# New engine orders for an attention and token-mixing kernel, its split last tile moved to the end of TensorE's list, and the tile's second half run as whole matmuls

## The chip, the cores and the metric

The kernel runs on one core of a Trainium2 chip. The metric is the device time of one execution in microseconds (us), measured over runs of the same program; it is compared between the kernel before and the kernel after. A difference of about half a per cent is the least that such a comparison can tell from none.

The engines have their own instruction lists and meet through semaphores: TensorE (PE, with its weight loads as PEld), VectorE (DVE), ScalarE (ACT), GpSimd (POOL) and SyncE (SP), which here only issues transfers.

## The reference

Two branches of one block read the same input x of 2048 tokens by 448 features and are mixed by a gate per token.

```python
def _A_ref(x, wq, wk, wv, wo, beta):          # 16 heads of 28, four segments of 512 tokens
    ...
    phi = lambda t: jnp.where(t > 0, t + 1.0, jnp.exp(t))
    ...
    for s in range(N):
        logits = jnp.einsum('bhqd,bhkd->bhqk', qs, ks) * scale + mask
        a_dot = jnp.einsum('bhqk,bhkd->bhqd', _softmax(logits, axis=-1), vs)
        ...
        a_mem = num / den                     # phi(q) @ M and phi(q) @ z, from the segments before
        o = g * a_mem + (1.0 - g) * a_dot
        M = M + jnp.einsum('bhld,bhle->bhde', pk, vs)
        ...
    return o @ wo

def _B_ref(x, w1, b1, w2, b2):                # an MLP over the tokens
    h = _layernorm(x, axis=-1)
    u = _gelu(jnp.einsum('bsd,sf->bdf', h, w1) + b1)
    return (jnp.einsum('bdf,fs->bds', u, w2) + b2).transpose(0, 2, 1)

g = _sigmoid((x * gate_w).sum(-1, keepdims=True))
return g * _A_ref(x, ...) + (1 - g) * _B_ref(x, ...)
```

## The kernel before

The program is a list of some 1,360 named steps. Each step knows its engine, what it reads and writes, and which PSUM bank it takes. `ORDER` is a table, written out by hand into the kernel, that says for every engine in which order its steps stand; `plan` reads it, and `finalize` turns dependencies into semaphore waits. Nothing is reordered at run time: each engine runs its list, and stops at a step whose inputs aren't there. In the table `u0-3*4` stands for the four steps u0-3 to u0-6, `@5` gives the PSUM bank that a step takes, and `#1` marks the second step of a name.

The names of the steps that matter here:

- `pr`, `lo`: projections to keys (k), queries (q) and values (t), on PE. `lo` are two matmuls of 64 rows side by side that begin two tiles at once; `pr` are the whole matmuls that end each of them. `prx`/`cpk1_3`/`cpq1_3` belong to the fourth group of heads, whose rows are gathered later.
- `cpk`, `cpq`, `cpv`: the copies of those results out of PSUM, on ACT or DVE (L703, L719, L765, L789 and others). `gt` is the gate's tanh. Some steps may stand on either engine; the table decides.
- `ek`, `mk`, `phk` and `eq`, `mq`, `phq`: the feature map phi of keys and queries (exponential on ACT, L748 and L772; then DVE).
- `sc0_0` to `sc7_4`: 40 scores steps (L942). Each fills the same four PSUM banks 0 to 3 with matmuls of 28 rows. `exp` (ACT, L951) reads the four banks in one instruction, and `mask` (POOL, L954) zeroes the triangle.
- `pv0` to `pv15`: probabilities times values (L972), in quarter matmuls; then on DVE `ta` (transpose out of PSUM, L986), `rec`, `oa`, `om`, `o` (L1000 on POOL, L1002 on DVE) and `ot` (L1007).
- `mem1` to `mem3` (L1018): phi(q) times the memory, into banks 0 to 3 too, taken out by `tm` on DVE (L1026) before the next scores. `mst` builds the memory.
- `u0` to `u13`: the first MLP product, 16 steps each; `gsq`, `gvh`, `garg`, `gth`, `gelu` work out the gelu.
- `y0` to `y15`: the second MLP product, 14 steps each, one tile of 128 tokens. `y15` is computed in two parts: columns 0 to 319 (`y15-0` to `y15-13`) and 320 to 447 (`y15-0#1` to `y15-13#1`). `wo` is the attention's output product and `ag` the copy that gates it. `fin` (DVE, L1096) adds both branches, and `out` stores them.
- `ldw1`, `ldw2`: loads of the MLP's weights into three slots on SP, each in four parts; `gk`, `gq`: the gathers of the fourth group's heads through a scratch buffer in DRAM; `gk3_h0` and `gk3_h1` bring back the keys of the last segment, which `sc7_2` is the first to read.

A step with mode "x" is either one matmul of 128 columns of weights (whole) or four of 32 columns (quarters, L264). `plan` makes all steps quarters that stand, without a step of narrower rows between, in one run with a `pv` or an `mst`.

Of the kernel before, what the change touches and what calls it, by code (L numbers as in the profile page):

```python
# [21 lines left out]
NFT = 14  # L22
# [266 lines left out]
btr@7 lok0_0 lok0_2 prk0_0 prx0_3 prk0_2 prk0_1 loq1_0@45 lok1_2@67 prk1_2 prq1_0 prq1_1 prx1_3 loq0_2 loq0_0  # L289
loq1_2@45 prq1_2h prq1_2 prq0_2 prq0_2h prq0_1 lot4@45 lot6@67 prq0_0 prt7 prt6 prt5 sc0_0 lok1_0@76 prk1_1 prk1_0  # L290
prt4 sc0_1 lok2_0@57 prk2_1 prk2_0 lok2_2@46 prx2_3 prk2_2 sc0_2 u0-0@5 u1-0@7*2 u2-0@4*2 u1-2*2 u0-1*5 u1-4*3 sc0_3
u0-6*4 u3-0@6*2 u1-7*2 u2-2*2 u0-10 u1-9*2 sc0_4 u2-4*3 u3-2 u0-11*5 u2-7*2 sc1_0 u1-11*5 u4-0@5 u2-9*2 u3-3*3
u4-1*3 u2-11*2 u3-6*2 pv0@7 sc1_1 u2-13*3 u3-8*6 u4-4*2 u3-14 u4-6 u3-15 u4-7*2 u6-0@7 u4-9*2 u5-0@4 u4-11 sc1_2
u4-12 u5-1*2 u4-13*3 u5-3 u6-1 u5-4*2 u6-2 u5-6 pv1@6 sc1_3 u5-7*4 u6-3*9 sc1_4 u5-11 u6-12*4 u7-0@5*3 u5-12*4
u7-3*2 u8-0@6 u7-5*2 sc2_0 u7-7*7 mst0@4 u8-1*3 sc2_1 u8-4*2 pv2@4 u7-14*2 u9-0@7*7 u8-6*2 sc2_2 loq2_0@45 prq2_1
prq2_0 u8-8*3 mem1 loq2_2@54 u8-11*3 prq2_2 u8-14*2 u9-7 prq2_2h u11-0@5*2 u9-8 u11-2*3 sc2_3 u9-9*4 pv3@4 u11-5*2
u10-0@6*2 u9-13*3 sc2_4 u11-7*3 u10-2 u12-0@4*3 u10-3 pv4@7 u12-3 u11-10*3 sc3_0 u11-13*3 u10-4*2 u13-0@7 u10-6*5
u12-4 sc3_1 u10-11*2 u13-1*2 u12-5 u10-13*3 pv5@5 u12-6 u13-3*2 u12-7*4 sc3_2 lot8@56 u13-5*2 u12-11*2 prt8 prt9
u12-13*2 sc3_3 u13-7*3 u12-15 u13-10 wo0#1@6 u13-11*4 mst1@5 u13-15 sc3_4 lok3_0@64 prk3_0 prk3_1 pv6@5 sc4_0
lot10@76 prt10 prt11 pv7@4 wo1@5 sc4_1 lok3_2@67 prk3_2 loq3_0@45 prq3_0 prx3_3 sc4_2 prq3_1 wo3@4 wo2@6 mem2  # L300
y0-0@5*4 y1-0@6*3 y0-4*4 y1-3*2 y0-8 sc4_3 loq3_2@47 y1-5*6 prq3_2 y1-11*2 sc4_4 y0-9 y1-13 y0-10*4 pv8@4 prq3_2h
sc5_0 y3-0@6*7 y2-0@7*3 y3-7 sc5_1 y2-3 wo5@5 y3-8*6 y2-4 sc5_2 y5-0@4*2 y2-5 pv9@5 wo4@6 y2-6 sc5_3 y5-2 y2-7 wo6@5
y2-8 wo7@6 sc5_4 y5-3*2 y2-9*3 y5-5*3 pv10@5 sc6_0 y5-8*3 y6-0@5 y2-12*2 y5-11*2 pv11@6 sc6_1 y5-13 y6-1*7 mst2@4
sc6_2 lot12@67 y4-0@4*2 prt13 y4-2 prt12 mem3 y6-8 y4-3 y6-9 y4-4*3 lot14@67 prt15 prt14 sc6_3 y4-7*5 y6-10*4
y4-12*2 sc6_4 wo8@6 y7-0@5*3 wo9@7 sc7_0 pv12@4 y7-3*4 wo11@6 sc7_1 y7-7*3 y9-0@4 pv13@7 y7-10*4 sc7_2 y8-0@7*4 y9-1
y8-4*4 y9-2*2 sc7_3 wo10@6 y8-8 pv14@5 y8-9*3 sc7_4 y10-0@5 y9-4 y11-0@6*2 y9-5*2 y10-1 y9-7 y8-12*2 y9-8 y11-2*5
y9-9*3 pv15@7 y10-2*3 y11-7*3 y10-5*2 y9-12*2 y11-10*2 y10-7*7 y11-12*2 wo15@7 y15-0@5*5 y15-0#1@6 y15-5*2 y15-1#1
# [36 lines left out]
mask4_2_2#1 mask4_4_1 mask4_4_3 mask4_3_0 mask5_1_1 mask5_0_0 mask5_1_3 mask5_2_2 mask5_2_2#1 o9 mask5_3_0 mask5_4_1
mask5_4_3 o10 mask6_0_0 o11 mask6_1_1 mask6_3_0 mask6_2_2 mask6_1_3 mask6_2_2#1 mask6_4_1 mask6_4_3 o12 mask7_0_0
mask7_1_1 mask7_1_3 mask7_2_2 mask7_2_2#1 o13 mask7_3_0 mask7_4_1 mask7_4_3""",
    "SP": """
dtx0_0 dtx0_1 ldwk0@0 ldwk1 ldwq0@1 ldwqb dtx1_0 dtx1_1 ldx0 ldx4 ldx8 ldbeta ldw1_0_0 dtx2_0 ldx12 dtx2_1 ldw1_0_1
ldw1_1_0 ldw1_0_2 tk0_0 gq0_1 ldw1_2_1 ldw1_1_2 gq0_0 gq0_3 gk0_2 gq0_2 ldw1_2_0 gk0_1 ldw1_1_1 gk0_0 gk0_3 ldw1_0_3
gq0_h1 ldw1_1_3 gq0_h2 gq0_h0 tk0_2 ldw1_3_1 gk0_h1 ldw1_2_2 gk0_h0 ldw1_3_0 ldw1_3_2 tk0_1 ldw1_2_3 gk2_0 tk1_0  # L350
ldw1_3_3 ldwo0 ldwo3 ldw1_4_2 ldw1_4_1 tk0_3 ldw1_4_0 ldwo0b ldwo1 ldw1_5_2 ldw1_5_0 ldwo1b gk2_1 ldw1_5_1 tk1_1
ldw1_5_3 ldw1_4_3 tk1_2 dtx3_0 gk2_2 ldw1_6_0 tk1_3 ldwo2 gq2_0 ldw1_6_1 ldw1_6_2 gq2_1 ldw1_6_3 ldwo2b gq2_3 gq2_2
gk2_3 gq2_h0 gq2_h1 gk2_h1 gq2_h2 ldw2_2_0 ldw2_0_1 dtx3_1 ldw2_2_2 tk2_1 ldw2_0_2 ldw2_1_0 tk2_0 gk2_h0 ldw2_1_1
ldw2_0_3 ldw2_1_2 ldw2_2_3 ldw2_0_0 ldw2_2_1 ldw2_1_3 gq3_3 gk3_3 out1 gq3_0 gq3_2 gk3_0 gq3_1 gk3_1 ldw2_3_0 tk2_3
gk3_2 out0 gq3_h1 gq3_h2 gk3_h0 ldw2_3_1 ldw2_3_3 gk3_h1 tk2_2 gq3_h0 out2 ldw2_3_2 ldw2_4_2 ldw2_5_0 ldw2_4_3
ldw2_4_0 ldw2_4_1 out4 out5 ldw2_6_0 ldw2_5_1 out3 out7 out6 ldw2_7_0 ldw2_5_2 ldw2_7_1 ldw2_5_3 ldw2_6_3 out8
ldw2_7_2 ldw2_7_3 ldw2_6_1 out10 out11 ldw2_6_2 out15 out9 out15#1 out14 out12 out13""",
}


def build_kernel(nc, X, WQ, WK, WV, WO, BETA, W1, B1, W2, B2, GW, OUT):
# [5 lines left out]
    out2 = OUT.rearrange("b s d -> (b s) d")  # L367
# [46 lines left out]
    uT = sb([128, NFT, D])  # L414
# [811 lines left out]
```

## Time and profile before

| | |
|---|---|
| median of 3 runs | 173.53 us (173.21 to 173.86) |
| the profiled execution | 173.38 us, of which 171.7 us are the profile's span |
| PE busy | 165.6 us, 96% of the span |
| DVE busy | 140.2 us, 82% |
| ACT busy | 132.5 us, 77% |
| POOL busy | 60.6 us, 35% |
| DMA | 25.17 MB moved, 147 GB/s on the mean |

The page divides the span into 40 slices, gives the chain of work that ended last, and groups of instructions by line. Its timeline gives for each group of neighbours the start, the duration and, in brackets, how long the engine sat idle before and what ended that. A matmul's shown duration reaches to its modelled end, so neighbouring matmuls overlap in the rows; from start to start shows the pace.

### The profile page before, as it was taken

How to read it: one execution, taken by the hardware profiler on the slowest of the kernel's cores; microseconds unless marked ns; L12 is line 12 of the kernel's file. 1: busy time of each engine (PE TensorE's matmuls, PEld its weight loads, DVE VectorE, ACT ScalarE, POOL GpSimd, SP SyncE). 2: the span in 40 equal slices, each digit the busy share in tenths (PEclk: the TensorE clock that was granted, in tenths of full speed). 3: DMA queues.
4: the chain of work that ended last, by engine and by line, in shares of the span. 5: the costliest groups of instructions: out<-in, count | busy, mean ns of one | idle time of the engine just before them, and what ended most of it. 6: DMA issues, size and time to landing. Idle time of an engine off the chain costs nothing.

```text
span 171.7 us, 5711 instructions
## 1 busy us (share of the span) xinstructions
PE 165.6 (96%) x2415; PEld 79.7 (46%) x2419; DVE 140.2 (82%) x322; ACT 132.5 (77%) x165; POOL 60.6 (35%) x94
## 2 busy tenths in 40 slices
PE   8799999999999999999999999999999999999992
PEld 2235333445444544544454335444544444566650
DVE  3088999979989899999999999987987777986103
ACT  0269999999999999999999998999895898501110
POOL 5000226441340009524255271467343848400000
PEclk9999999999999999999999999999999999999999
DMA  6999995779895695610539900173346150574212
GB/s 145 260 263 288 240 207 156 211 199 223 201 209 157 162 169 132 201 32 15 144 103 203 289 4 0 39 109 115 96 126 197 49 174 28 168 227 122 85 38 80
DMA packets 52632, 25.17 MB, mean 147 GB/s; under 512 B 17134, under 2 KB 52366, under 8 KB 52606
## 3 DMA queue, kind: packets, MB, share of 16 engines
q1 hardware_dynamic: 51814, 24.22, 57.7%
q10 hardware_dynamic: 792, 0.58, 1.7%
q8 instruction: 19, 0.31, 0.9%
q14 instruction: 7, 0.06, 0.1%
HBM read 18.76 MB, written 2.36 MB: 123 GB/s over the span
## 4 chain that ended last, share of the span: by engine, by line
PE 85%; DVE 5%; SPq 5%; DMA 3%; issue 1%
PE t L264 71%; PE t L942 7%; PE t L972 5%; SPq L516 4%; DMA t<-in_A_x_dram 3%; DVE t L885 2%; DVE t L1026 1%; PE t L825 1%; SPq L506 1%; PE t L1018 1%; DVE t L719 1%; DVE t L1096 0%; DVE t L752 0%; SPq L510 0%; DVE t L763 0%
## 5 line engine op out<-in xcount | busy, mean ns | idle before, releaser
L264 PE MATMUL t<-t 128*32 128x448 bf16 (+8 forms) x1650 | 141.7, 347 | 2.1 <-DMA t<-in_A_wv_dram 0.8
L264 PEld LDWEIGHTS t<-t 128*32 128x32 bf16 (+2 forms) x1654 | 64.8, 97 | 64.7 <-issue 14.1
L951 ACT ACTIVATE t<-t 128x2048 bf16<-128x2048 f32 x40 | 75.1, 1877 | 5.6 <-PE t L942 5.0
L954 POOL TENSOR_SCALAR_AFFINE_SELECT t<-t 128x512 bf16<-128x512 bf16 x64 | 43.7, 699 | 51.5 <-ACT t L951 44.8
L1050 ACT ACTIVATE t<-t 128x448 bf16<-128x448 f32 x14 | 10.1, 725 | 13.4 <-DVE t L911 7.6
L1096 DVE SCALAR_TENSOR_TENSOR t<-t 128x448 bf16<-128x448 f32 (+2 forms) x17 | 10.7, 644 | 9.2 <-PE t L264 9.2
L1000 POOL TENSOR_TENSOR t<-t 128x448 bf16<-128x448 f32 x9 | 10.7, 1184 | 14.9 <-DVE t L998 8.3
L942 PE MATMUL t<-t 28*128 28x512 bf16 (+3 forms) x256 | 15.8, 301 | 0.0
L986 DVE STREAM_TRANSPOSE t<-t 128x512 f32<-128x512 f32 x16 | 11.4, 713 | 3.8 <-PE t L972 3.8
L894 POOL TENSOR_TENSOR t<-t 128x4 f32<-128x4 f32 x4 | 4.1, 1032 | 22.2 <-DVE t L892 22.2
L1007 DVE STREAM_TRANSPOSE t<-t 128x512 bf16<-128x512 bf16 x16 | 11.0, 690 | 1.1 <-POOL t L1000 1.0
L972 PE MATMUL t<-t 128*32 128x512 bf16 (+3 forms) x256 | 11.5, 300 | 0.0
L942 PEld LDWEIGHTS t<-t 28*128 28x128 bf16 x256 | 4.4, 92 | 13.2 <-ACT t L951 6.3
L787 ACT ACTIVATE t<-t 128x448 bf16<-128x448 f32 x12 | 6.4, 546 | 4.5 <-PE t L264 4.5
L885 DVE BATCH_NORM_STATS2 t<-t 128x6 f32<-128x448 bf16 x16 | 9.2, 608 | 0.8 <-DMA t<-in_A_x_dram 0.8
L1076 DVE SCALAR_TENSOR_TENSOR t<-t 128x448 f32<-128x448 f32 x14 | 9.6, 684 | 0.2
L972 PEld LDWEIGHTS t<-t 128*32 128x32 bf16 x256 | 6.7, 97 | 5.6 <-POOL t L954 0.6
L1068 ACT ACTIVATE t<-t 128x448 f32<-128x448 f32 x14 | 8.8, 633 | 0.4 <-PE t L264 0.3
L996 DVE SCALAR_TENSOR_TENSOR t<-t 128x448 f32<-128x448 f32 x12 | 8.9, 739 | 0.1
L748 ACT ACTIVATE t<-t 128x512 bf16<-128x512 bf16 x12 | 7.6, 631 | 1.4 <-DVE t L705 1.4
L1081 DVE SCALAR_TENSOR_TENSOR t<-t 128x448 bf16<-128x448 f32 x14 | 8.5, 610 | 0.0
L752 DVE SCALAR_TENSOR_TENSOR t<-t 128x512 bf16<-128x512 bf16 x12 | 8.4, 703 | 0.1
(75 smaller groups left out, 129.9 us busy)
## 6 DMA issues: line engine op xcount, KB each, us to landing
t<-in_B_w_dram SPq DMA_DIRECT2D x52, 256.0 KB, 3.7
t<-in_A_x_dram SPq DMA_DIRECT2D x4, 448.0 KB, 4.6
out_dram<-t SPq DMA_DIRECT2D x15, 112.0 KB, 3.2
t<-in_B_w_dram SPq DMA_DIRECT2D x8, 128.0 KB, 3.7
t<-in_A_wv_dram ACTq DMA_DIRECT2D x4, 112.0 KB, 4.1
t<-in_A_wq_dram SPq DMA_DIRECT2D x1, 336.0 KB, 5.0
spare_heads<-t SPq DMA_DIRECT2D x8, 32.0 KB
spare_heads<-t SPq DMA_DIRECT2D x16, 16.0 KB
```

The source lines that it names most:

```text
L264: last = e.matmul(out[q], w[:, q], x, skip_group_check=True, **kw)
L885: op("DVE", lambda e: e.bn_stats(st6[:, t, :], xh[:, t, :]), reads=[R_x[t]], writes=[R_st6[t]], name=f"bns{t}", cost=512, prio=P_PROJ - 10 ...
L942: last = e.matmul(bank(hl)[:, c0 : c0 + w], kT[r, hg, s * 512 + j * 128 : s * 512 + j * 128 + 128], qT[r, hg, s * 512 + 128 * j : s * 512 ...
L951: op("ACT", lambda e: e.activation(pslot(g), ps[:, 0:4, :], ACT.Exp, scale=SCALE), reads=R_bank[0:4], writes=[g.res], take=g, name=f"exp{p ...
L954: op("POOL", lambda e, c0=c0: e.affine_select(pslot(g)[:, :, c0 : c0 + 128], pslot(g)[:, :, c0 : c0 + 128], pattern=[[0, 4], [1, 128]], co ...
L972: last = e.matmul(bank(cb)[32 * ((hl + hg) % 4) : 32 * ((hl + hg) % 4) + 32, 128 * j : 512], vaug[:, 4 * s + j, 32 * h : 32 * h + 32], psl ...
L986: dv(lambda e: e.transpose(tt[:, ia, :], bank(cb)[:, 0:512]), [bres(cb)], [R_tt[ia]], "ta", 630, use=(cb,))
L1000: op("POOL", lambda e: e.tensor_tensor(o3, n3[0], n3[1], op=ALU.add), reads=[R_tt[ia], R_tt[im]], writes=[R_ob[tb]], name=f"o{u}", cost=12 ...
L1007: dv(lambda e: e.transpose(oT[:, hg, s * 512 : s * 512 + 512], o), [R_ob[tb]], qres(hg, s), "ot", 635)
L1050: op("ACT", lambda e: e.activation(ag(T), bank(b)[:, 0:D], ACT.Identity, bias=b2g[:, T : T + 1], scale=gcol[:, T : T + 1]), **buse(b), rea ...
L1076: op("DVE", lambda e: e.scalar_tensor_tensor(gg[:, q, :], gg[:, q, :], 1.0, vh[:, q, :], op0=ALU.add, op1=ALU.mult), reads=[R_gg[q], R_vh[ ...
L1096: op("DVE", lambda e: e.scalar_tensor_tensor(outst[:, p, c0:c1], bank(b)[:, 0 : c1 - c0], omg[:, T : T + 1], ag(T)[:, c0:c1], op0=ALU.mult ...
```

## The change

It has two parts. The first replaces `ORDER` by another table: the same steps, except that some which may stand on two engines change engine. From ACT to DVE go cpq0_1, cpk1_0, cpv4, cpv11, ag0, ag4, ag5, ag9, ag11 and ag12; from DVE to ACT go the second cpq1_2, cpq1_3, cpv5, cpk2_3, gvh0, cpq2_2, cpv10 and ag8; o8 goes from DVE to POOL, o9 and o12 come the other way. The second part is one expression in `mm2`: the second part of the last tile (`c0` is 320) is never split into quarters.

```diff
 ORDER = {
     "PE": """
...
-btr@7 lok0_0 lok0_2 prk0_0 prx0_3 prk0_2 prk0_1 loq1_0@45 lok1_2@67 prk1_2 prq1_0 prq1_1 prx1_3 loq0_2 loq0_0
-loq1_2@45 prq1_2h prq1_2 prq0_2 prq0_2h prq0_1 lot4@45 lot6@67 prq0_0 prt7 prt6 prt5 sc0_0 lok1_0@76 prk1_1 prk1_0
+btr@7 lok0_0 lok0_2 prk0_0 prx0_3 prk0_2 prk0_1 lok1_2@45 loq1_0@67 prk1_2 prq1_0 prx1_3 prq1_1 loq1_2@46 loq0_0
+loq0_2 prq0_2 prq1_2 prq0_1 prq0_2h prq1_2h prq0_0 lot4@45 lot6@67 prt7 prt6 sc0_0 prt4 prt5 lok1_0@67 prk1_0 prk1_1
...
-y15-10#1 y15-11#1 y15-12#1 y14-0@7 y15-13#1 y12-5 y14-1*2 y12-6 y14-3*3 wo13@5 y13-0@6*3 y14-6*2 y13-3 y12-7 y13-4*3
-y12-8*5 y14-8*6 y12-13 y13-7*7""",
+y13-10 y14-12*2 y12-2*3 y13-11*2 y12-5 y13-13 y12-6*8 y15-7*7 y15-0#1@5 y15-1#1 y15-2#1 y15-3#1 y15-4#1 y15-5#1
+y15-6#1 y15-7#1 y15-8#1 y15-9#1 y15-10#1 y15-11#1 y15-12#1 y15-13#1""",
...
     "SP": """
...
-gk3_2 out0 gq3_h1 gq3_h2 gk3_h0 ldw2_3_1 ldw2_3_3 gk3_h1 tk2_2 gq3_h0 out2 ldw2_3_2 ldw2_4_2 ldw2_5_0 ldw2_4_3
+gq3_h2 tk2_2 gk3_1 ldw2_4_0 out0 ldw2_4_1 ldw2_3_2 gq3_h0 ldw2_4_2 gq3_h1 ldw2_3_3 gk3_2 out3 out2 ldw2_4_3 gk3_h0
+out4 gk3_h1 out5 ldw2_5_0 ldw2_5_1 ldw2_5_3 ldw2_7_0 ldw2_5_2 ldw2_6_2 out6 ldw2_6_0 ldw2_7_2 out7 ldw2_6_1 ldw2_7_3
...
@@ def mm2(T, c0=0, c1=D):
-                                                     uT[:, ft, c0:c1], cols, start=(ft == 0), stop=(ft == NFT - 1)),
+                                                     uT[:, ft, c0:c1], cols and not c0, start=(ft == 0), stop=(ft == NFT - 1)),
```

Lines below the table have numbers one less in the kernel after, since its table is a line shorter.

On ACT, in the first 20 us, the copies of keys and queries stand like this before (L703 and L717 copy keys and the fourth group, L765 queries, L748 and L772 are exponentials of the feature map):

```order
L717 ACTIVATE t<-t 128x512
L748 ACTIVATE t<-t 128x512
L717 ACTIVATE t<-t 128x512
L765 ACTIVATE t<-t 128x512 x2
L772 ACTIVATE t<-t 128x512
L703 ACTIVATE t<-t 128x512
L765 ACTIVATE t<-t 128x256
L717 ACTIVATE t<-t 128x512
L772 ACTIVATE t<-t 128x512
L765 ACTIVATE t<-t 128x256 x2
```

and like this after:

```order
L716 ACTIVATE t<-t 128x512
L702 ACTIVATE t<-t 128x512
L764 ACTIVATE t<-t 128x512
L716 ACTIVATE t<-t 128x512 x2
L747 ACTIVATE t<-t 128x512
L716 ACTIVATE t<-t 128x512
L764 ACTIVATE t<-t 128x256 x2
L764 ACTIVATE t<-t 128x512
L764 ACTIVATE t<-t 128x256 x2
L764 ACTIVATE t<-t 128x512
```

The two exponentials of queries (L772: eq1_1 and eq1_0) have moved out from among the copies, the copy of keys (L703, now L702: cpk1_2) has moved ahead, and one more copy of the fourth group (L716: cpq1_3) stands here that stood on DVE.

On PE, around 107 us, with the scores of fills 5_0 to 5_2 (L942; the rows of 384 and 128 columns are one step), before:

```order
L942 MATMUL t<-t 128x512 x4
L264 MATMUL t<-t 128x448 x11
L942 MATMUL t<-t 128x384 x4
L942 MATMUL t<-t 128x128 x4
L264 MATMUL t<-t 128x448 x12
L942 MATMUL t<-t 128x256 x8
```

and after:

```order
L941 MATMUL t<-t 128x512 x4
L264 MATMUL t<-t 128x448 x10
L941 MATMUL t<-t 128x384 x4
L941 MATMUL t<-t 128x128 x4
L264 MATMUL t<-t 128x448 x10
L941 MATMUL t<-t 128x256 x8
```

Ten whole matmuls stand between one scores step and the next, where eleven and twelve stood.

At the end of PE's list (quarters of 32 columns of weights; 448, 320 or 128 columns of data), before:

```order
L264 MATMUL t<-t 32x448 x24
L264 MATMUL t<-t 32x128 x4
L264 MATMUL t<-t 32x448 x12
L264 MATMUL t<-t 32x128 x40
L264 MATMUL t<-t 32x448 x4
L264 MATMUL t<-t 32x128 x4
L264 MATMUL t<-t 32x448 x160
```

and after:

```order
L264 MATMUL t<-t 32x448 x72
L264 MATMUL t<-t 32x320 x4
L264 MATMUL t<-t 32x448 x84
L264 MATMUL t<-t 32x320 x28
L264 MATMUL t<-t 128x128 x14
```

The second part of y15, fourteen steps of 128 columns, has moved from among y12's and wo's steps to the very end, as fourteen whole matmuls instead of 56 quarters.

More of the change, by code (lines that the diff above doesn't have):

```diff
@@ L298 @@
[L298 to L307, printed above, removed]
@@ new lines @@
+prq3_2h y1-9*2 y0-8 y1-11*3 sc4_4 y0-9*5 y3-0@7 pv8@4 y2-0@5*2 sc5_0 y3-1 y2-2*2 y3-2*2 y2-4 y3-4*4 sc5_1 y2-5*4
+wo5@4 y3-8*2 sc5_2 pv9@6 y3-10*3 wo4@4 y3-13 sc5_3 y2-9*3 y5-0@6 y2-12*2 wo6@7 sc5_4 y5-1*4 wo7@4 pv10@5 sc6_0
+y5-5*8 pv11@4 sc6_1 mst2@5 y5-13 y6-0@7*7 sc6_2 lot12@45 prt12 y6-7*2 prt13 y6-9*2 mem3 lot14@64 prt14 prt15 y6-11*3
+y4-0@6*3 sc6_3 y4-3*11 sc6_4 wo9@4 y7-0@5*2 wo8@6 sc7_0 pv12@7 y7-2*2 wo11@4 y7-4*2 sc7_1 y9-0@7*2 pv13@4 y7-6*4
+y8-0@6 sc7_2 y8-1 y7-10*4 y8-2*2 y9-2*2 y8-4 y9-4 sc7_3 y9-5*3 wo10@4 pv14@5 y8-5 sc7_4 y8-6*3 y9-8 y11-0@5 y8-9*3
@@ new lines @@
+y9-9*3 y8-12*2 y11-1*7 pv15@4 y10-0@6 y11-8*5 y9-12*2 y10-1*5 y11-13 y10-6*8 wo15@4 wo13@5 wo14@6 y14-0@7*4
+y15-0@4*3 y14-4 y15-3*2 y13-0@5 y14-5 y15-5 y13-1*2 y14-6 y13-3*2 y14-7*5 wo12@6 y13-5*4 y15-6 y13-9 y12-0@6*2
+y13-10 y14-12*2 y12-2*3 y13-11*2 y12-5 y13-13 y12-6*8 y15-7*7 y15-0#1@5 y15-1#1 y15-2#1 y15-3#1 y15-4#1 y15-5#1
+y15-6#1 y15-7#1 y15-8#1 y15-9#1 y15-10#1 y15-11#1 y15-12#1 y15-13#1""",
+    "ACT": """
+ldwv0 ldgw ldwv1 ldwv2 ldwvb ldwkb ldb1 ldb2 cpv2 cpv0 gt0 gt2 cpv1 gt3 gt1 ek0_0 cpk0_1 cpk0_3 cpk1_2 cpq1_0 cpq0_3
@@ new lines @@
+ta10 rec10 oa10 om10 o9 ta11 msta2 rec11 mstc2 ot9 fin5 mq3_3 om11 phq3_3 oa11 tm13 tm12 tm15 tm14 ot10 gcol3 ot11
+fin4 gcol2 fin6 omg2 b2g2 eps13 omg3 b2g3 ag9 eps14 eps12 ta12 rec12 ag11 eps15 om12 oa12 o12 ta13 rec13 ot12 om13
+fin7 oa13 ta14 rec14 oa14 om14 ot13 fin8 o14 ot14 ta15 rec15 om15 oa15 o15 ot15 fin11 fin10 fin9 ag14 ag12 fin14
+fin13 fin12 fin15 fin15#1""",
+    "POOL": """
+szb szg mhalf oo0 og0 id0 oo1 v0 v1 og1 id1 oo2 rstd0 mask0_0_0 rstd4 rstd8 og2 mask0_1_1 mask0_1_3 rstd12 mask0_3_0
```

92 lines of the change are left out of this document (43 added, 49 removed).

## The prediction

> **What bounds the kernel now.** I read the page first, then the busy time by stretch, then the chain that ended last, then single places in the timeline.
>
> ```profile
> PE 165.6 (96%) x2415; PEld 79.7 (46%) x2419; DVE 140.2 (82%) x322; ACT 132.5 (77%) x165; POOL 60.6 (35%) x94
> ...
> DVE  3088999979989899999999999987987777986103
> ...
> PEclk9999999999999999999999999999999999999999
> ...
> PE 85%; DVE 5%; SPq 5%; DMA 3%; issue 1%
> ```
>
> ```profile
> 0.00:18.78 18.78, 16.67 (x84) 6.65 (x86) 10.50 (x34) 9.57 (x22) 3.10 (x16) 1.00 0.98 238
> 18.78:168.57 149.79, 148.90 (x2332) 73.05 (x2335) 129.01 (x288) 122.91 (x144) 57.46 (x79) 1.00 0.56 136
> 168.57:171.66 3.09, 0.00 (x0) 0.00 (x0) 0.68 (x1) 0.00 (x0) 0.00 (x0) 0.99 0.33 111
> ```
>
> TensorE (PE) is the bound, at full clock. From 18.78 to 168.57 us it is busy for 148.90 of 149.79 us, and 85% of the chain is its own work. A new order can take away only what isn't matmul work: PE's waits, and the 3.09 us after the last matmul. The wait ahead of 18.78 is the largest.
>
> ```profile
> 18.04 0.68 DVE L719 CAST t<-t 128x512 bf16<-128x512 f32 x1
> 18.18 0.10 PEld L264 LDWEIGHTS t<-t 64*128 64x128 bf16 x2 [0.46 <-DVE t L763]
> 18.78 0.36 PE L264 MATMUL t<-t 64*128 64x449 bf16 x2 [0.23 <-DVE t L719]
> ```
>
> **What a unit of PE work costs.** The chain gives it by differences.
>
> ```profile
> 107.60 0.33 PE t L942 x4
> 107.92 2.19 PE t L264 x11
> 110.11 0.33 PE t L942 x8
> 110.44 2.38 PE t L264 x12
> ...
> 140.28 0.76 PE t L264 x16
> ```
>
> Twelve whole matmuls of 448 columns take 2.38 us, eleven 2.19: 0.19 each, and 2.19 - 11 x 0.19 = 0.10 is left for the change of array rows after a scores step (L942, 0.33). Sixteen quarter matmuls (four units) take 0.76: 0.19 a unit too. Whole or in quarters costs the same, so that the new order runs more units whole is worth nothing. Both orders hold the same 627 named PE steps, and by my count of the two lists as many changes between 128-row and narrower tiles (112). PE's pure work is unchanged; waits and end remain.
>
> **Waits that go.** Where the previous step started, and what that step needs elsewhere, gives each wait.
>
> ```profile
> 87.54 0.40 PE L942 MATMUL t<-t 28*128 28x384 bf16 x8
> 88.05 0.72 PE L264 MATMUL t<-t 64*128 64x512 bf16 x6
> 102.35 0.39 PE L942 MATMUL t<-t 28*128 28x512 bf16 x4
> 102.92 0.28 PE L264 MATMUL t<-t 64*128 64x256 bf16 x2 [0.17 <-DVE t L719]
> 145.99 0.40 PE L942 MATMUL t<-t 28*128 28x384 bf16 x8
> 146.40 0.74 PE L264 MATMUL t<-t 128*32 128x448 bf16 x10
> 150.07 0.15 PEld L972 LDWEIGHTS t<-t 128*32 128x32 bf16 x8 [0.33 <-POOL t L954]
> 154.70 0.12 PEld L264 LDWEIGHTS t<-t 128*32 128x32 bf16 x8 [0.34 <-DVE t L1007]
> ```
>
> - lot6 at 18.78: its pair lot4 loads weights at 18.18, so 0.60 from step to step where 0.19 is due: 0.41. It waits for cpq1_3 (L719) on VectorE. In the new order it needs cpq1_1 and the second cpq1_2, on ScalarE, with the queries' exponentials (eq1_1, eq1_0) gone from among those copies, and prq1_2h and prq0_0 stand ahead of lot4. Of the nine copies from cpk1_2 to the second cpq1_2, the last has its input when prq1_2h ends. After that come prq0_0 (three matmuls of 512 columns, 0.19 x 512/448 = 0.22 each), a change of rows (0.10) and lot4 (0.19): 0.9 us until lot6 is due, for a copy of 0.38 by the row below. The wait goes.
>
> ```profile
> 16.95 0.38 ACT L765 ACTIVATE t<-t 128x256 bf16<-128x256 f32 x1 [0.16 <-PE t L264]
> ```
>
> - loq3_2 at 102.92: 0.57 after sc4_3 where 0.33 is due: 0.24. It waits for cpq3_3, queued on VectorE behind the four transposes after mem2. The new order puts 17 units instead of 14 between mem2 and sc4_3: 0.57 more cover. It goes.
> - lok3_0 at 88.05: 0.51 against 0.33, so 0.18; y10-0 at 146.40: 0.41, so 0.08. The units between a bank's last use and its next use grow in the new order (from pv14 to the next tile in its bank 1.0 to 1.4 us at 0.19 a unit). Both go.
> - Four small ones, two of them the last two rows (pv15 on a mask, wo15 on ot15), the others at u11-0 and y6-0. The rows show only that a weight load sat idle for 0.33 to 0.34. Bounds by the places above: 0.08 and 0.24; I take 0.12 each, nearer to 146.40, since no PE idle stands in those rows: 0.5. In the new order pv15 has 20 units ahead of it instead of 19, and wo15 comes 22 instead of 21 after pv15: 0.19 more, enough for both.
>
> Sum: 0.41 + 0.24 + 0.18 + 0.08 + 0.5 = 1.41 us less.
>
> **Waits that come.** A scores step writes the four banks that the exponential reads, so the next scores step must wait for that.
>
> ```profile
> 115.25 0.39 PE L942 MATMUL t<-t 28*128 28x512 bf16 x4
> 115.80 1.87 ACT L951 ACTIVATE t<-t 128x2048 bf16<-128x2048 f32 x1
> 117.76 0.40 PE L942 MATMUL t<-t 28*128 28x384 bf16 x8
> ```
>
> 2.51 us from scores to scores, of which only 0.09 lies between the end of the exponential (117.67) and the next scores: the shortest possible distance is about 2.42. Before, eleven units stand there: 0.33 + 0.10 + 11 x 0.19 = 2.52. After, five stretches (from sc5_0, sc5_1, sc5_3, sc6_4 and sc7_1) hold work for ten: 2.33, so PE waits 0.1 in each: 0.5 us. Ends: 0.3 and 0.7, since each is a difference of rounded rows. Nothing is made up later, as PE has no other idle time.
>
> Copies moved between engines: ten leave ScalarE for VectorE and eight go the other way, o9 and o12 come to VectorE from GpSimd and o8 leaves. Net about 3 us more on VectorE, at 0.6 to 0.7 each. They lie beside PE as long as VectorE keeps its lead (129.01 of 149.79 busy). If not, a bank comes free late, and matmuls wait as at 102.92. No row shows these new places: between 0 and as much as goes (1.41). I take 0.2, nearer to nothing, because almost all distances between uses of a bank grow.
>
> DMA: the loads of weights and the gathers are reordered, in the same number. Cover: the last W2 part for y14 and y15, now behind out8, leaves by my estimate 4 us ahead of its use (fin8 is done by then, y9's last matmul comes 2 us after pv15, and wo15, wo13, wo14 and seven units stand between), and weights land like this:
>
> ```profile
> DMA to landing us min/median/max: 2.4/3.7/6.1
> ```
>
> So the median is covered and the longest isn't: 0 to 2 us. I take 0, nearest to the median. What a gather without cover costs is the third rival.
>
> **The end.** Before, the last tile is y13, 448 columns: copy 0.68 (L1096), then a store. After, it is the 128-column half of y15. The lines are, in this order, from the chain, the answer for the copy's line (shortest, median and longest in ns), the page's DMA issues (last number: us to landing), the groups by shape (last number but one: ns of one), and the last store before.
>
> ```profile
> 168.59 0.68 DVE t L1096
> ...
> L1096 DVE SCALAR_TENSOR_TENSOR t<-t x17: 352/673/685, 106.2 to 168.6; 128x448 bf16<-128x448 f32 x15, 128x128 bf16<-128x128 f32 x1, 128x320 bf16<-128x320 f32 x1
> ...
> out_dram<-t SPq DMA_DIRECT2D x1, 32.0 KB, 1.6
> ...
> L264 PE MATMUL t<-t 128*32 128x448 bf16 x1076 | 56.8, 353 | 0.0
> ...
> L264 PE MATMUL t<-t 128*32 128x128 bf16 x56 | 1.6, 219 | 0.0
> ...
> DMA to landing us min/median/max: 1.7/1.7/1.7
> ```
>
> A matmul's latency beyond its own columns is alike (353 - 190 and 219 - 55 ns), so the end shortens by the copy, 0.68 - 0.35 = 0.33, and the landing, 1.7 - 1.6 = 0.10: 0.43 us. The copies of y12 and of y15's first half are done when the last result is there (14 x 0.055 = 0.77 us and the latency cover them).
>
> Whole instead of quarter matmuls at 128 columns: no row has a run of them. By columns 0.19 x 128/448 = 0.055 each, as in quarters. Below that the rows leave no room. Above: the mean weight load, 98 ns, if each matmul had to wait for its own weights: 14 x 0.043 = 0.6 us more.
>
> ```profile
> L264 PEld LDWEIGHTS t<-t 128*128 128x128 bf16 x358 | 32.0, 98 | 35.0 <-issue 7.4 <-DVE t L634 0.5 <-DMA t<-in_A_x_dram 0.4
> ...
> 4.48 0.17 PE L808 MATMUL t<-t 128*128 128x3 bf16 x1
> 4.51 0.16 PE L809 MATMUL t<-t 128*128 128x1 bf16 x1
> 4.53 0.38 PE L623 MATMUL t<-const-bfloat16-1.0 128*128 128x512 bf16 x1
> ```
>
> I take 0.055: three whole matmuls, each with weights of its own, start 0.03 apart here, so weights don't hold the pace. One change from quarters to whole without a scores step between is new; ends 0 and 0.2, and I take the 0.10 of the change above.
> The Trainium skill, TensorE: Matmul & The Clock Gate, section Back-to-back issue gap, speaks against this: it gives about 81 ns per matmul in a stream of weight loads and matmuls at N=128, by which the half tile would cost 14 x 0.026 = 0.36 us more. The same sentence gives about 131 ns at N=512, where the trace needs 0.19 us for 448 columns, so the trace doesn't bear it out.
>
> **Sum** on the profiled execution (173.38 us, 1.72 outside its span of 171.66): -1.41 + 0.5 + 0.2 - 0.43 + 0.10 = -1.04, so 172.3. The median of the runs is 0.15 higher (173.53): 172.5.
>
> **Rivals.**
> 1. New waits replace the old ones. VectorE is busy for eight or nine tenths of nearly every slice up to 107 us (DVE on the page, 25 slices of 4.3 us) and gets 3 us more; against it stand the longer bank distances. With half to all of the 1.41 given back: 173.0 to 173.7.
> 2. The half tile runs at the pace of its weight loads: 172.5 + 0.6 = 173.1, and with half of that 172.8. For it: PEld's 98 ns; against it: the three starts 0.03 apart. By the section of the Trainium skill named above it would be 172.9.
> 3. Slower: the last gather of keys, gk3_h1, now stands on SP behind out4, which waits for fin4. In before's times fin4 ends 133.9 (row below), so the gather leaves at about 134.5; sc7_2 needs it, at 140.97 before and some 0.2 earlier after, 6.2 us later. Weight loads land in 6.1 at the longest, but this gather shows no landing. Beyond 6.2 us each us is one of PE: a landing after 7.2 takes the gain, one after 8.2 gives 172.5 + 2.0 = 174.5. Before, it stood ahead of out2, out4 and out5 on SP.
>
> ```profile
> 133.18 0.69 DVE L1096 SCALAR_TENSOR_TENSOR t<-t 128x448 bf16<-128x448 f32 x1 [1.17 <-PE t L264]
> 140.97 0.40 PE L942 MATMUL t<-t 28*128 28x256 bf16 x8
> ```
>
> **How the numbers follow.** Forecast 0.60 (171.8 to 172.9), rival 1 0.22, rival 2 0.10, rival 3 0.08. About 0.5% (0.87 us) is what a measurement of this kernel can tell from no change. The forecast lies under 172.66 in about five of six cases: faster 0.50. The rest of it and rivals 1 and 2 make same, 0.42; rival 3 is slower, 0.08. The range, 171.7 to 173.6, holds the forecast, rival 2 and nearly all of rival 1; rival 3 lies outside, and my bounds for the new waits and the weight loads are too rough to draw it closer.
>
> **What would show it.** No PE wait at lot6 and its cast; scores to scores 2.4 us with ten units between in the five stretches; PE's idle time between 18 us and its end about 0.9 us less; the last copy 0.35 and about 2.65 us from last matmul to the end; fourteen matmuls 128x128 within 0.8 us. The prediction is wrong if waits on VectorE (L986, L1026, L719) show at new places, if those fourteen spread over 1.1 us or more, or if scores at L942 wait for a DMA.

## The result, and the profile after

| | before | after |
|---|---|---|
| runs of one comparison | 173.61 us median (173.21 to 174.22, 6 runs) | 171.75 us median (171.35 to 172.21, 6 runs) |
| ratio | | 0.989, 95% interval 0.9866 to 0.9914 |
| profiled execution | 173.38 us, span 171.66 | 171.96 us, span 170.2 |

The kernel became 1.86 us faster; 172.5 was forecast, 171.7 to 173.6 the range, so the result stands at its lower end. The page of the kernel after, then its busy time by stretch (before the wait that was at lot6, up to the last matmul, and behind it; columns as in the prediction: TensorE, its weight loads, VectorE, ScalarE, GpSimd, granted clock, DMA share, GB/s):

```profile
PE 166.1 (98%) x2319; PEld 79.8 (47%) x2323; DVE 140.1 (82%) x325; ACT 130.7 (77%) x163; POOL 58.8 (35%) x93
...
PEclk9999999999999999999999999999999999999999
...
PE 94%; DMA 3%; ACTq 1%; issue 1%; POOL 0%; DVE 0%; POOLq 0%
```

```profile
18.48:167.88 149.40, 148.91 (x2239) 72.77 (x2240) 129.70 (x295) 121.62 (x143) 56.46 (x77) 1.00 0.58 139
167.88:170.20 2.32, 0.00 (x0) 0.00 (x0) 0.35 (x1) 0.00 (x0) 0.00 (x0) 1.00 0.23 65
```

TensorE keeps its full clock. Its share of the chain rose from 85 to 94%: the links over VectorE and over SyncE's queue (5% each) are gone. The last row stops at 170.20, the span at 170.23: from the end of the last matmul to the end of the span it is 2.36 us, and 3.12 by the same reading before. The wait at lot6 is gone too; in the timeline of TensorE of after, the matmuls run through that place:

```profile
16.77 3.42 PE L264 MATMUL t<-t 128*128 128x256 bf16 x21
```

The starts of scores steps with ten units between them (L941 is the scores' line in after):

```profile
107.49 0.39 PE L941 MATMUL t<-t 28*128 28x512 bf16 x4
107.81 2.06 PE L264 MATMUL t<-t 128*128 128x448 bf16 x10
109.87 0.40 PE L941 MATMUL t<-t 28*128 28x384 bf16 x8
110.20 2.07 PE L264 MATMUL t<-t 128*128 128x448 bf16 x10
112.25 0.40 PE L941 MATMUL t<-t 28*128 28x256 bf16 x8
```

Scores to scores is 2.38 us, at 107.49, 109.87 and 112.25, where 2.33 is due: the exponential now sets the pace there, at a cost of 0.05 a stretch. The one that starts at 107.93 ends at 109.81, 0.06 ahead of the next scores (ScalarE):

```profile
107.93 1.88 ACT L950 ACTIVATE t<-t 128x2048 bf16<-128x2048 f32 x1 [0.62 <-PE t L941]
```

At one scores step, sc6_3, it is not the exponential but the transposes that empty the banks after mem3 (L1025, the last ends at 130.26):

```profile
130.31 0.10 PEld L941 LDWEIGHTS t<-t 28*128 28x128 bf16 x4 [0.41 <-DVE t L1025]
```

The end of after, from the timeline and the answer for the stores' line:

```profile
166.91 0.78 PEld L264 LDWEIGHTS t<-t 128*128 128x128 bf16 x14 [0.27 <-DVE t L1095]
167.04 0.55 DVE L1095 SCALAR_TENSOR_TENSOR t<-t 128x320 bf16<-128x320 f32 x1 [0.27 <-PE t L264]
167.91 0.35 DVE L1095 SCALAR_TENSOR_TENSOR t<-t 128x128 bf16<-128x128 f32 x1 [0.32 <-PE t L264]
```

```profile
DMA to landing us min/median/max: 1.5/1.5/1.5
```

The fourteen weight loads of the whole half tile fit into 0.78 us; the copy takes 0.35 and the store lands after 1.5 us, where 0.68 and 1.7 stood before.

The sum over all steps of TensorE, each placed by the order of its list, and each time from one step's start to the next less the unit costs of the prediction:

| term, us | predicted | in the trace of after |
|---|---|---|
| waits of before that went | -1.41 | -1.58 |
| waits for the exponential at scores | +0.5 | +0.29 (five of 0.05 to 0.07) |
| new waits elsewhere | +0.2 | +0.19 (0.14 at prt10, behind mst1; 0.05 at sc6_3, behind mem3) |
| quarters to whole | +0.10 | +0.11 |
| whole matmuls of 128 columns | 0 (0.055 each) | 0 (0.056 each) |
| end | -0.43 | -0.77 |
| sum | -1.04 | -1.76 |

The first 10 us, a start that the change leaves alone up to lok0_0, vary by themselves: lok0_0 began between 10.15 and 10.77 us in all the profiles of this case, at 10.37 in before's and 10.72 in after's. From there to the end of the span it is 161.3 us before and 159.5 after, 1.8 less, which agrees with the medians.

### The profile page after: what moved, and what is told of

Read it like the earlier page. It is cut to its first block, busy times and chain, and to the rows that moved or that the text cites. A ratio compares the mean times of both kernels' runs of the same rounds, so it can differ in the third digit from the quotient of the medians.

```text
span 170.2 us, 5519 instructions
## 1 busy us (share of the span) xinstructions
PE 166.1 (98%) x2319; PEld 79.8 (47%) x2323; DVE 140.1 (82%) x325; ACT 130.7 (77%) x163; POOL 58.8 (35%) x93
## 3 DMA queue, kind: packets, MB, share of 16 engines
HBM read 18.76 MB, written 2.36 MB: 124 GB/s over the span
## 4 chain that ended last, share of the span: by engine, by line
PE 94%; DMA 3%; ACTq 1%; issue 1%; POOL 0%; DVE 0%; POOLq 0%
PE t L264 79%; PE t L941 8%; PE t L971 5%; DMA t<-in_A_wv_dram 3%; PE t L824 1%; PE t L1017 1%; ACTq L505 1%; ACTq L526 0%; DVE t L1095 0%; POOL t L524 0%; POOL t L591 0%; POOL t L567 0%; POOL t L590 0%; POOL t L584 0%; POOLq L1210 0%
## 5 line engine op out<-in xcount | busy, mean ns | idle before, releaser
L264 PE MATMUL t<-t 128*32 128x448 bf16 (+9 forms) x1554 | 141.6, 351 | 1.0 <-issue 0.6
L953 POOL TENSOR_SCALAR_AFFINE_SELECT t<-t 128x512 bf16<-128x512 bf16 x64 | 42.6, 680 | 52.7 <-ACT t L950 51.5
L941 PE MATMUL t<-t 28*128 28x512 bf16 (+3 forms) x256 | 15.8, 301 | 0.0
L999 POOL TENSOR_TENSOR t<-t 128x448 bf16<-128x448 f32 x8 | 9.8, 1220 | 16.4 <-DVE t L995 8.4
L1049 ACT ACTIVATE t<-t 128x448 bf16<-128x448 f32 x9 | 6.5, 722 | 7.4 <-PE t L264 7.3
L941 PEld LDWEIGHTS t<-t 28*128 28x128 bf16 x256 | 4.5, 92 | 14.0 <-ACT t L950 7.1
L786 ACT ACTIVATE t<-t 128x448 bf16<-128x448 f32 x12 | 6.4, 544 | 4.1 <-PE t L264 4.0
L1053 DVE TENSOR_SCALAR t<-t 128x448 bf16<-128x448 f32 x7 | 5.2, 740 | 5.1 <-PE t L264 5.0
L995 DVE SCALAR_TENSOR_TENSOR t<-t 128x448 f32<-128x448 f32 x12 | 8.8, 731 | 0.1
L1075 DVE SCALAR_TENSOR_TENSOR t<-t 128x448 f32<-128x448 f32 x14 | 8.5, 615 | 0.1
```

The source lines that it names most:

```text
L264: last = e.matmul(out[q], w[:, q], x, skip_group_check=True, **kw)
L941: last = e.matmul(bank(hl)[:, c0 : c0 + w], kT[r, hg, s * 512 + j * 128 : s * 512 + j * 128 + 128], qT[r, hg, s * 512 + 128 * j : s * 512 ...
L953: op("POOL", lambda e, c0=c0: e.affine_select(pslot(g)[:, :, c0 : c0 + 128], pslot(g)[:, :, c0 : c0 + 128], pattern=[[0, 4], [1, 128]], co ...
L995: dv(lambda e: e.scalar_tensor_tensor(n3[0], n3[0], oc, rb[0], op0=ALU.mult, op1=ALU.mult), [R_tt[ia], R_rec[tb], R_omcol], [R_tt[ia]], "o ...
L999: op("POOL", lambda e: e.tensor_tensor(o3, n3[0], n3[1], op=ALU.add), reads=[R_tt[ia], R_tt[im]], writes=[R_ob[tb]], name=f"o{u}", cost=12 ...
```

## Experiments: the end

The expectations count the experiments in the order in which they ran: their first is the old order with the new end, their sixth the one at u11-0 and loq3_2.

**The changed kernel with its end undone.**

```diff
 PE:  ... y13-13
-y12-6*8 y15-7*7 y15-0#1@5 ... y15-13#1
+y15-7*7 y15-0#1@5 ... y15-13#1 y12-6*8
 DVE: -... fin12 fin15 fin15#1   +... fin15 fin15#1 fin12
 SP:  -... out12 out15 out15#1   +... out15 out15#1 out12
-uT[:, ft, c0:c1], cols and not c0,
+uT[:, ft, c0:c1], cols,
```

> The changed kernel with its end undone: the same order, but both parts of y15 stand ahead of the last eight units of y12, all in quarters, so that a copy and a store of 448 columns come last, as in before. If the end is worth what the traces show (copy 0.33, landing 0.2, four more waits of SyncE at 0.06 behind the last store's, and no change of mode, 0.11 less): 0.66 more, 172.4 beside 171.75. By the prediction's terms (0.43, less 0.10): 172.1. If the end is worth nothing: 171.75.

172.38 us (6 runs), ratio to before 0.9934 (0.992 to 0.9947): 0.63 slower than the changed kernel, and 1.05 slower than the changed kernel in quarters (below), which ran in the same comparison. Its last stretch, and the answer for the last store:

```profile
167.54:170.70 3.16, 0.00 (x0) 0.00 (x0) 0.68 (x1) 0.00 (x0) 0.00 (x0) 1.00 0.11 36
```

```profile
DMA to landing us min/median/max: 1.7/1.7/1.7
```

3.16 against 2.36 is 0.80, less the change of mode that is saved (0.11): 0.69 by the traces. In the runs it is 0.63 or more; either way it is more than the 0.33 of the prediction's two terms.

**The old order with the new end.**

```diff
 PE:  -... y15-0#1@6 ... y15-13#1 in eight places between y15-4 and y12-5
      +... y13-7*7 y15-0#1@5 y15-1#1 ... y15-13#1
 DVE: fin15#1 last   SP: out15#1 last
+uT[:, ft, c0:c1], cols and not c0,
```

> The order of before, with only the end of the new order: the 128-column half of y15 last on TensorE as fourteen whole matmuls, its copy last on VectorE, its store last on SyncE. If the end is worth what the two traces show from the last matmul to the end of the span (2.32 us after, 3.09 before, so 0.77 less) and the change from quarters to whole matmuls costs its 0.11, this kernel is 0.66 us under before: about 172.95 beside 173.6. By the prediction's own terms (0.43 less, 0.10 more) it is 0.33 under: 173.3. Rival: all of the gain comes from TensorE's waits, and the end is worth nothing: 173.6.

173.38 us (12 runs) beside 173.67, ratio 0.9988 (0.9974 to 1.0002): less than expected, and not told apart from nothing. Its last stretch and, from the timeline, the weight loads at u0-12:

```profile
168.93:171.40 2.47, 0.00 (x0) 0.00 (x0) 0.35 (x1) 0.00 (x0) 0.00 (x0) 1.00 0.35 107
```

```profile
35.65 0.49 PEld L264 LDWEIGHTS t<-t 128*128 128x128 bf16 x4 [0.56 <-DMA t<-in_B_w_dram]
```

From the last matmul's end to the end of the span at 171.36 it is 2.44 us, 0.68 less than before's 3.12, so the gain is there in this order too. Of it 0.11 goes into the change of mode, 0.06 into a new wait at y14-0 (its bank came free late, since the units of y15 no longer lay between), and 0.30 into a wait for the load of W1 at u0-12, which has nothing to do with the end; the wait at lot6 was 0.14 smaller. That makes 0.35 less; from lok0_0 to the end of the span it is 160.9 us, 0.37 less than before.

**The second edit undone alone.**

```diff
-uT[:, ft, c0:c1], cols and not c0,
+uT[:, ft, c0:c1], cols,
```

> The changed kernel with the second edit undone: its order is unchanged, but the last 128-column half of y15 runs in quarters like the tiles ahead of it, 56 small matmuls instead of fourteen whole ones. If whole and quarter matmuls cost the same by columns and the change from the one to the other costs 0.11 us: 171.65 beside the 171.75 of the changed kernel. If the change of mode costs nothing in the end: 171.75. If whole matmuls are what makes the end short (quarters 0.04 each more): 172.3.

171.33 us (5 runs), ratio 0.9879 (0.9862 to 0.9896). The intervals overlap with the changed kernel's, so the runs don't tell the two apart. The traces do: y15-13 to the first step of the second half takes 0.11 more in after and nothing more here, and the units of the second half follow each other in 56 ns in both. The edit to whole matmuls costs 0.11 us, and brings back 0.03 at most: from the last matmul's end to the end of the span it is 2.39 here.

**SyncE's last waits reversed, in the changed kernel.**

```diff
-for sp2 in sorted(sch.out_spaces):
+for sp2 in sorted(sch.out_spaces, reverse=True):
```

> The changed kernel, in which SyncE at the very end waits for the seventeen stores in the reverse order, so that sixteen waits, all of them for stores that have landed, stand behind the wait for the last store instead of none. If each costs the 0.06 us that lay between such waits at the end of before: 0.95 more, 172.7 beside 171.75. Rival: waits for what has come cost nothing that the time shows: 171.75.

171.44 us (6 runs), ratio 0.9876 (0.9853 to 0.9898). The expectation's premise didn't hold: the compiled program takes two semaphores in one wait and had paired them so that the last store was again in the last one, here in the branch that ends the row. So sixteen waits behind the last store were not tried. The run is one more sample of the new order: with the kernel in quarters and the changed kernel, 171.3 to 171.75.

## Experiments: where a wait goes when it is taken away

**lot6.** One step moved in the old order:

```diff
-prq0_1 lot4@45 lot6@67 prq0_0 prt7
+prq0_1 prq0_0 lot4@45 lot6@67 prt7
```

> The order of before, with one step moved: prq0_0 (three matmuls of 512 columns, 0.66 us) stands ahead of lot4 and lot6 on TensorE instead of behind them, so that the wait of 0.41 us at lot6 has other work in its place. If a wait taken from TensorE shows in full in the time: 0.41 less, 173.2 beside 173.6. Rival: VectorE and ScalarE, which set the next waits, come no earlier, and what lot6 no longer waits is waited at u11-0, sc0_0 or lok2_0 instead: 173.6, with their waits (0.25, 0 and 0.06 in before) larger by 0.41 together.

173.29 us (12 runs) beside 173.67, ratio 0.9983 (0.9973 to 0.9994). The trace takes the rival's side; TensorE and its weight loads in the timeline:

```profile
24.27 0.93 PE L264 MATMUL t<-t 64*128 64x512 bf16 x4 [0.34 <-ACT t L703]
...
32.01 1.63 PEld L264 LDWEIGHTS t<-t 128*128 128x128 bf16 x10 [0.39 <-DVE t L901]
```

lot6 no longer waits, but lok2_0 waits 0.41 us instead of 0.06, for the copy cpk1_0 that stands on ScalarE behind the first exponential and a gate step, and u0-9 waits 0.11 for its layer norm (L901) on VectorE. From lok0_0 to the last step it is 157.85 us, 157.81 in before. So nothing was gained in the profiled execution; that the runs are some 0.3 faster was not explained (the loads below were one try). The traces can hardly show it, since the profiled execution of before, with 173.38, lies 0.3 under the median it is compared with here, and this kernel's, with 173.22, only 0.1.

**u11-0 and loq3_2.**

```diff
-prq2_2h u11-0@5*2 u9-8 u11-2*3 sc2_3 u9-9*4 pv3@4
+prq2_2h u9-8*3 u11-0@5*3 sc2_3 u11-3*2 u9-11*2 pv3@4
...
-sc4_3 loq3_2@47 y1-5*6 prq3_2
+y1-5*2 sc4_3 loq3_2@47 y1-7*4 prq3_2
```

> The order of before with units moved at two waits of TensorE: three units of u9 stand ahead of u11-0 (which waited 0.25 us for the copy cpq2_2), and two units of y1 stand ahead of sc4_3 and loq3_2 (which waited 0.24 us for the copy cpq3_3). If waits in the stretch after 35 us, where TensorE is the only bound, are taken away for good: 0.49 less, 173.15 beside 173.65. Rival: they are given back at later waits, as the one at lot6 was in its trace: 173.65.

173.69 us (12 runs) beside 173.55, ratio 1.0009 (0.9991 to 1.0026): nothing gained. Both waits are gone from their places, and stand at others (TensorE, then VectorE):

```profile
68.02 0.39 PE L942 MATMUL t<-t 28*128 28x512 bf16 x4 [0.18 <-DVE t L1026]
...
105.36 0.40 PE L942 MATMUL t<-t 28*128 28x384 bf16 x8 [0.20 <-ACT t L951]
...
66.73 1.24 DVE L1026 STREAM_TRANSPOSE t<-t 128x512 f32<-128x512 f32 x2
```

In before the first and the last of these rows read:

```profile
68.08 0.39 PE L942 MATMUL t<-t 28*128 28x512 bf16 x4
...
66.78 1.24 DVE L1026 STREAM_TRANSPOSE t<-t 128x512 f32<-128x512 f32 x2
```

sc2_3 needs the four transposes (L1026) that take mem1 out of the scores' banks; the last ends at 67.97, and the scores start at 68.02. In before they started at 68.08, 0.06 behind the same transpose: u11-0's wait was only where this chain showed. And with two units fewer between them, sc4_4 had to wait for the exponential of sc4_3 (2.37 us from scores to scores). In this execution mem2 came 0.15 later as well, since the exponential of sc4_1 started 0.4 later, and y0-0 behind it waited 0.12; lot6 waited 0.14 less. From lok0_0 to the last step it is 157.97 us, 0.16 more than in before.

**u11-0 again, with work for the whole chain.** Two more units ahead of sc2_3, taken from the stretch behind it, where before had 0.74 us between the exponential and the next scores:

```diff
-prq2_2h u11-0@5*2 u9-8 u11-2*3 sc2_3 u9-9*4 pv3@4
+prq2_2h u9-8*3 u11-0@5*3 u9-11*2 sc2_3 u11-3*2 pv3@4
```

> The order of before with the wait at u11-0 (0.25 us) treated again: as in the sixth experiment three units of u9 stand ahead of u11-0, and now two more units stand ahead of sc2_3, taken from behind it. Theory: sc2_3 can't start before the last of the four transposes that follow mem1 on VectorE (it ended at 68.02, sc2_3 began at 68.08 in before, 67.97 and 68.03 in the sixth experiment), so that u11-0's wait was only the place where this shows; with 0.38 us more work in that stretch the wait goes for good: 173.3 beside 173.55, no wait at u11-0 or sc2_3, and sc2_4 no later than before. Rival: it is given back at sc2_4 or later: 173.55.

173.29 us (12 runs) beside 173.66, ratio 0.997 (0.9954 to 0.9986). Scores on TensorE, in the timeline:

```profile
68.40 0.40 PE L942 MATMUL t<-t 28*128 28x512 bf16 x4
...
71.09 0.40 PE L942 MATMUL t<-t 28*128 28x384 bf16 x8
```

No wait at u11-0 or sc2_3, and sc2_4 as early as before though lok0_0 began 0.19 later. From lok0_0 to the last step: 157.57 us, 0.24 less than before, with a wait of 0.09 for a load at u0-12 in it and 0.06 less at lot6. This is what the new order does at both places: it puts 15 units instead of 12 between mem1 and sc2_3, and 17 instead of 14 between mem2 and sc4_3, so that the transposes are done when the scores come (67.58 for 67.93, 101.92 for 102.55).

## Experiments: the loads of W1

**One load moved ahead, in the old order; and the same with the new end.**

```diff
 SP:
-ldw1_0_2 tk0_0 ... gk0_0 gk0_3 ldw1_0_3 gq0_h1
+ldw1_0_2 ldw1_0_3 tk0_0 ... gk0_0 gk0_3 gq0_h1
```

> The order of before with one load moved: the last quarter of the first W1 part (ldw1_0_3) stands on SyncE behind ldw1_0_2 instead of behind nine gathers of queries and keys. In the profiled execution of before it left at 31.57 us, landed 3.5 us later and was needed at 35.48; in the profile of before with the new end it left at 31.44, took 4.2 us, and TensorE waited 0.30 us for it at u0-12. Theory: most executions of before wait there for some 0.3 us which its profiled one just missed, and the 0.38 us that the kernel with prq0_0 moved gained in its median came from there (its load left at 30.26): this kernel is 0.3 under before, 173.35 beside 173.65. Rival: that gain came from the wait at lot6, and the load costs nothing in most executions: 173.65.

> The order of before with the new end (as in the first experiment, with y14-0 one unit later, so that it doesn't wait for its bank) and with ldw1_0_3 early on SyncE. Theory: the end is worth 0.66 here as it is in the changed kernel, and gave only 0.29 since the wait at u0-12 was larger by 0.30 in that profile and y14-0 waited 0.06; with the load early 0.3 more: 172.7 beside 173.65. Rival: in before's order the end is worth no more than the 0.29 that was measured, and the load nothing: 173.35.

173.87 us (12 runs, up to 174.76) beside 173.55, ratio 1.002 (0.9998 to 1.0043); with the end, 173.79 (12 runs, up to 175.02), ratio 1.002 (1.0 to 1.004). Both theories fell: neither is faster than before, and the new end shows no gain in the second. Its timeline shows why:

```profile
35.21 2.06 PE L264 MATMUL t<-t 128*128 128x448 bf16 x10 [0.76 <-DMA t<-in_B_w_dram]
```

That is u2-4, which waits 0.83 us for ldw1_1_1. In before that load left SyncE at 29.96 us and landed 0.91 before its use. With another load ahead of it, it left at 31.50 here; in the profile of the first of the two kernels it left at 30.32 and landed 0.53 before its use.

**Two pairs of loads exchanged,** so that nothing stands later than before except loads with time to spare.

```diff
 SP:
-tk0_0 gq0_1 ldw1_2_1 ldw1_1_2 ... gk0_1 ldw1_1_1 gk0_0 gk0_3 ldw1_0_3
+tk0_0 gq0_1 ldw1_0_3 ldw1_1_1 ... gk0_1 ldw1_1_2 gk0_0 gk0_3 ldw1_2_1
```

> The order of before with two pairs of loads exchanged on SyncE, so that the queue holds no more work at any place: ldw1_0_3 (landed 0.40 us before its use in the profile of before, later than its use in that of the first experiment) takes the place of ldw1_2_1 (15.0 us before its use), and ldw1_1_1 (0.86) that of ldw1_1_2 (7.6). Theory: most executions of before wait for one of these two loads, some 0.3 us in the median, and moving one load ahead alone only made the other late (0.83 us of wait at u2-4): with both early and nothing delayed this kernel is 0.3 under before, 173.25 beside 173.55, and its runs spread less than before's 1.2 us. Rival: the loads cost nothing in the median, and what the kernel with prq0_0 moved gained (0.38) was the wait at lot6: 173.55.

173.39 us (12 runs, 173.03 to 174.11) beside 173.66, ratio 0.9997 (0.9978 to 1.0015). The loads now land 7.6 and 5.8 us before their use, and the time is not told apart from before, the spread little smaller. So a late load of W1 can cost 0.3 us in a single execution (as at u0-12 above) and 0.8 where one is pushed back. That they cost 0.3 in the median of before is neither shown nor ruled out: the medians lie 0.27 apart, and the interval reaches from 0.4 less to 0.3 more.

## Experiments: half of each order

```diff
 all engines: [steps begun before sc3_4, as in the one order] + [the rest, as in the other]
```

> Half of each order: all engines follow the new order up to the fill sc3_4 (some 86 us), and the old one from there on, the old end with it. The waits of before that lie ahead of sc3_4 are 0.41 (lot6), 0.06 and 0.25 (u11-0): if these go, and the two loads of W1 no longer come late (0.3 in the median), 172.55 beside 173.55; by the waits alone 172.85. Rival: since single waits there were given back when one was taken away, the early half gains nothing: 173.55.

> The other half: the old order up to sc3_4, the new one from there on, with the new end. The end is worth 0.63 (measured on the changed kernel), the waits of the late half 0.82 less in before against 0.34 at the scores and 0.02 to 0.14 at prt10 that come: 0.34 to 0.46 less; together 172.5 beside 173.55. If the early half gains nothing (rival above), the whole gain lies here: 171.75. If the late waits that go and come are equal, 172.9.

177.57 us (6 runs, 176.03 to 178.56), ratio 1.0208 (1.0164 to 1.0252), and 176.35 us (6 runs, 174.8 to 177.97), ratio 1.0129 (1.0091 to 1.0167). Both are slower than either whole order, by a wait at the seam (sc3_4, where the one order follows the other) that neither has. New order first, TensorE's timeline and the stretches behind it:

```profile
89.43 0.94 PE L264 MATMUL t<-t 128*32 128x448 bf16 x16 [3.37 <-DVE t L1085]
```

```profile
89.43:90.43 1.00, 1.00 (x47) 0.68 (x48) 0.60 (x1) 0.01 (x1) 0.00 (x0) 1.00 0.79 224
90.43:93.85 3.42, 3.42 (x85) 1.41 (x71) 0.69 (x2) 2.60 (x2) 0.40 (x1) 0.50 1.52 261
93.85:96.00 2.15, 2.15 (x42) 0.95 (x38) 1.31 (x4) 1.33 (x2) 2.08 (x4) 0.99 0.75 121
96.00:100.00 4.00, 4.00 (x69) 1.70 (x58) 4.00 (x9) 4.00 (x7) 1.03 (x2) 1.00 0.75 180
```

wo0 needs a bank that gvh12 (L1085) empties, and gvh12 stands on VectorE behind a step that waits, through ScalarE, for a gather. In the other kernel the wait at the seam is 2.34 us:

```profile
89.21 2.66 PE L264 MATMUL t<-t 128*128 128x448 bf16 x30 [2.34 <-DVE t L1086]
```

The halves' times therefore don't divide the gain. What the traces still show: from lok0_0 to the seam the new order had no wait of TensorE over 0.02 us; in the other kernel the late half of the new order had the same six waits at scores as in after, 0.04 to 0.07, and none of the seven that the old late half has (0.03 to 0.24). Added up from the traces of before and after, the waits that went are worth 0.76 ahead of sc3_4 and 0.82 behind it, where 0.48 comes back.

## Why the prediction was right, and where not

- **The end** is the term that was mis-sized: 0.43 predicted, 0.77 in the trace, and by the kernel with its end undone 0.63 in the runs net of the change of mode, for which 0.33 was due (1.05 against the kernel in quarters, for which 0.43 was due). The copy was right (0.68 to 0.35). The landing went from 1.7 to 1.5 us instead of to the 1.6 taken from the earlier store of the same size: 0.1 more. The last 0.2 lies behind the landing: SyncE waits for the stores in a fixed order, and in before the store that landed last was followed by three more waits, at 171.06, 171.12 and 171.18 us in its records, and a branch; in after the branch follows at once. Across the traces the time from the last landing to the end of the span grows with the waits behind it: 0.42 us where that store's wait is in the branch itself (the waits reversed), 0.48 to 0.49 with none behind (after, and four kernels more with the new end), 0.66 to 0.67 with three (before, and six kernels more with its end), 0.73 with four (the end undone), so some 0.06 each. The prediction had no term for this.
- **Waits that go** were right in kind and sum: 0.41, 0.24, 0.18, 0.08 and four of 0.08 to 0.25 (0.5 taken together, 0.53 measured), and three that weren't listed, lot4, lok2_0 and mem3 (0.14 together). TensorE's idle time from 18 us to its last matmul, for which 0.9 less was forecast, fell from 1.10 to 0.48 us, 0.62 less. That the four small ones came out so close is in part luck: the one at u11-0 was 0.25, twice what was assumed, and the other three less. The reason given was too simple. The prediction treated each as a stall of TensorE alone, and the experiments show that taken one by one the waits at lot6, u11-0 and loq3_2 come back at the next step of the same chain. In after they are gone, with the work of ScalarE and VectorE moved and more units in the chain; that it takes work for the whole chain is shown for u11-0 by the two more units ahead of sc2_3, and argued from the trace of after for lot6 and loq3_2. The prediction had seen that for loq3_2 (17 units instead of 14 behind mem2), and not that it was the same chain at u11-0, for which it assumed 0.12.
- **Scores' pace:** 0.29 instead of 0.5. The shortest distance was taken as 2.42 from a pair whose exponential started 0.56 after the scores; with a start after 0.45, as in most pairs, and the 0.06 that stay between the exponential and the next scores in all five stretches, it is 2.38.
- **New waits,** 0.2: 0.14 at prt10 behind mst1 in the profile of after, 0.02 to 0.13 in three other profiles of the new order, and 0.05 at sc6_3 for the transposes behind mem3, a new place of the kind that the prediction had named as a sign against it. The 3 us more on VectorE didn't show at all: with three instructions more its busy time is 140.1 us on the page of after and 140.2 on that of before.
- **Loads:** 0, as taken. The last W2 part behind out8 left 4.3 us ahead of its use, where 4 was estimated, and landed 1.6 ahead of it.
- **Change of mode:** 0.10 predicted, 0.11 measured. **Whole matmuls:** 0.055 and 0.056. The ground for this, three starts 0.03 apart, was thin: in after the first two of the same three matmuls start 0.07 apart. The figure of about 81 ns in the Trainium skill (TensorE: Matmul & The Clock Gate, section Back-to-back issue gap) is not what a stream of weight loads and matmuls of 128 columns took here; the formula for a single matmul's gap in the same section, which gives 56 ns, is.
- **Rivals.** New waits in place of the old ones (the first) held in part: 0.48 of 1.58 came back, less than the half that was its condition. The second, weight loads as the pace, is ruled out by the fourteen loads in 0.78 us and matmuls 56 ns apart. The third did not come: the gather gk3_h1 left at 134.0 us, 6.1 ahead of sc7_2, and sc7_2 started 0.06 behind the exponential before it, and no scores step waited for a transfer.

The errors in the end, in the waits that went and in the scores' pace all point the same way, which is why the time came out 0.75 us under the forecast. Open are the 0.3 us by which the runs with prq0_0 moved were faster than their trace says, and how the gain of the runs divides between the early and the late half of the order, beyond the sum of waits in two traces.

## What to carry to other kernels

A wait of the bounding engine is worth its length only if the work behind it, on the engines that it waits for, also comes earlier; find the next step that needs the same chain, and see whether there is work to fill the chain to its end. Of a last tile, make the last piece small and count what follows it to the end of the program, not the copy alone. A table of orders that was found as a whole need not come apart: split at one step here, each half was slower than either whole order.

## What the runs showed of the hardware

- A pause of TensorE can have a second price: after 3.37 us of waiting the granted clock was 1.00 for 1 us more, then 0.50 for 3.42 us (90.43 to 93.85), and 1.00 after that; after 2.34 us in the other half kernel it stayed 1.00 in the profile. The Trainium skill (TensorE: Matmul & The Clock Gate, section What's actually happening) gives an idle window of about 3.4 us before the clock is halved; the trace agrees with it, as far as these two pauses show.
- The same start of the program varies by 0.6 us from one execution to the next (lok0_0 from 10.15 to 10.77), more than most of the terms above.
